# A third of the gated layer's seven products computed by halves, and the guard's maxima replaced by sums of squares on ScalarE

## The chip, the cores and the metric

The kernel runs on one core of a Trainium2 chip. A core has TensorE (PE in the profile; its weight loads are PEld), VectorE (DVE), ScalarE (ACT), GpSimd (POOL) and SyncE (SP), each with an instruction queue of its own, and 16 DMA engines that the queues of SP, ACT and POOL feed. The metric is the device time of one execution in microseconds (us), the median of the runs.

## The reference

Attention in which a query sees only the keys whose 6 hash bits equal its own, then a layer with a squared ReLU, in float32:

```
mask   = q_bucket[:, :, :, None] == k_bucket[:, :, None, :]     # 4 x 8 heads, 768 x 768
scores = where(mask, q @ k.T / 8, -1e9)
x      = softmax(scores) @ v        # as 3072 tokens x 512
h      = x @ w_in                   # 512 x 2048
g      = max(h, 0) ** 2
out    = g @ w_out                  # 2048 x 512
```

## The kernel before

All engines work in the order in which the program is written (a manual schedule); tile pools put in the waits. A tile name with `bufs=n` has n buffers, and a new tile of that name waits until an older one is done with.

**Attention** comes first (0 to 320.9 us). Its softmax leaves out the subtraction of the row's maximum. That is sound if scores stay small, so a guard looks at all of q and k: `load_peak` loads them in 32 pieces (through GpSimd's queue, two buffers `raw_qk`), `peak` takes the largest absolute value of each piece on VectorE, `tops` and `guard` reduce these, and a slow general path at the end is taken if the bound fails.

**The layer** runs over three chunks of 1024 tokens. Both of its products are matrix products by halves: each operand is cut in 2 x 2 blocks, and seven products of blocks, or of sums and differences of blocks, stand for the eight plain ones. The seven are numbered 0 to 6 in the code (`at(0)` to `at(6)`), and their results are added up in this way: "one" is product 0, "two" is 0 + 4, "five" is 3, "three" is "two" + 5; the four blocks of the result are 0 + 1, "two" + 3 + 6, "three" + "five", and "three" + product 2. TensorE adds in its accumulators (`acc0`, `acc1`, `acc2`, two buffers each), ScalarE copies what has to be kept on the way (`keep`: one, two, three, five), and VectorE adds (`gate_sum`) and makes the squared ReLU (`gated`).

*First layer, chunk 0* (`hidden`, 320.9 to 417.2 us): eight units r, each of seven products of two matmuls with 512 columns.

*First layer, chunks 1 and 2* (`hidden_pair`): the eight units are taken in four pairs; pair n holds units n (half 0) and n + 4 (half 1). Products 0, 3, 4, 5, 6 of each unit are "outer" matmuls with 512 columns, two for each product. Products 1 and 2 are computed for both units of a pair at once, by halves once more: seven "inner" matmuls with 256 columns take the place of eight such. `inner_steps` makes the steps 0 to 3 of an inner product and `put`, which adds it to a kept sum and gates it; `snaps` holds its kept copies. The inner weights are made once, in chunk 0's second layer, by `factor_units`, stored in `w_in_49`, and loaded by `load_inner`; `sums_inner` makes the differences of x. `load_unit` loads the outer weights. After each half, VectorE makes differences of the results (`minus` into `b_t` and `b12`), after each pair a slice of those for the second layer (`inner_sums(0, ...)`), and two `peak`s.

*Second layer* (`project`, k = 0 to 6): seven outer products, each of seven inner ones (`product`), each of these four matmuls with 256 columns on a quarter of `b11` ... `b_t`, with weight tiles `leaf` (seven buffers, loaded through ScalarE's queue). In `product` the groups go in the order 0, 1, 4, 3, 5, 6, 2. Group 4 needs `t2` of `inner_sums`, and the last one ("t4") needs `y21 - t2`, which VectorE makes in `hook`, called after the second group. The order around the change on VectorE in chunk 0 is: the sums of `factor_units(k - 1)` for k = 1 to 4, `hook`, the adds of the seven results (`first_`, `seventh`, ...), then differences for later k. `factor_units` loads its two sources and stores its results through GpSimd's queue, in tiles named `h` (five buffers), which the gating and `put_out` use too. `put_out` stores results mainly through SP's queue.

The functions in the code:

Of the kernel before, what the change touches and what calls it, by code (L numbers as in the profile page):

```python
# [34 lines left out]
def kernel(  # L35
# [49 lines left out]
    w_in_49 = p_d.tile([NQ, P, 2, 7, P], FP32, name="w_in_49")  # L85
# [572 lines left out]
    with tc.manual_schedule():  # L658
# [168 lines left out]

        def product(n, w, at, bt, c11, c12, c21, c22, hook=None):
# [47 lines left out]
        def peak(i):  # L876

            nc.vector.tensor_reduce(  # L878
                out=peaks[:, :, i], in_=raw_qk.pop(i), axis=AXL.X, op=ALU.max,
                apply_absolute_value=True,  # L880
            )
# [9 lines left out]
        def guard():  # L891
# [3 lines left out]
            for w in range(2):  # L895
# [8 lines left out]
                out=slow, in0=most[:, 0:1], scalar1=most[:, 1:2], scalar2=PLAIN / (scale * D),  # L904
# [52 lines left out]

        def factor_units(n):

            src = [new_h().rearrange("p (a f c) -> p a f c", a=2, c=P) for _ in range(2)]  # L960
            for j in range(2):
                nc.gpsimd.dma_start(out=src[j], in_=w_in_7[j * NQ + n, :, 5:7])
            sums = [new_h().rearrange("p (a f c) -> p a f c", a=2, c=P) for _ in range(2)]
            sums_a(
                src[0][:, :, 0], src[0][:, :, 1], src[1][:, :, 0], src[1][:, :, 1],
                *(sums[j // 2][:, :, j % 2] for j in range(4)),
            )
            for lo, hi, t in (
                (0, 2, src[0]), (2, 3, src[1][:, :, 1:2]), (3, 5, sums[0]), (5, 7, sums[1])
            ):  # L970
                nc.gpsimd.dma_start(out=w_in_49[n, :, :, lo:hi], in_=t)

        def load_inner(i, n):

            if n < NQ:
                w_inner[i, n] = []
                for j, name in enumerate((("sum0", "sum3"), ("sum2", "sum1"))[n % 2]):
                    t = p_y.tile([P, 4, QN], FP32, name=name).rearrange("p a (b c) -> p (a b) c", c=P)
                    nc.sync.dma_start(out=t[:, 0:7], in_=w_in_49[n, :, j])
                    w_inner[i, n].append(t)  # L980

        def quarters_x(i, j):

            b = xs[i][0][:, 2:4, 0:HN] if j == 0 else xs[i][0][:, 0:2, HN:NCH]
            return b[:, 0, 0:QN], b[:, 0, QN:HN], b[:, 1, 0:QN], b[:, 1, QN:HN]

        def sums_inner(i):

            t_inner[i] = [p_y.tile([P, NQ, QN], FP32, name=f"t{m}", bufs=2) for m in range(2)]
# [7 lines left out]
        def inner_steps(i, n, j):  # L997
# [5 lines left out]
            if i not in snaps:  # L1003
                o = [p_y.tile([P, HN], FP32, name="o", bufs=NOUT) for _ in range(2)]
                snaps[i] = [o[m // 2][:, m % 2 * QN:(m % 2 + 1) * QN] for m in range(4)]
            one, two, three, five = snaps[i]

            def mul(out, a, b, start, stop):
                nc.tensor.matmul(  # L1009
                    out=out, lhsT=w[:, a], rhs=b, start=start, stop=stop, skip_group_check=True  # L1010
                )
# [10 lines left out]
            def step_1():  # L1022
                hs["a2"] = spare("acc3")[:, 0, 0:QN]
# [24 lines left out]
        def hidden_pair(i, n, half):  # L1048

            r = half * NQ + n  # L1050
            w, bt = w_unit.pop(i * NR + 2 * n + half), factors_x(i)
            acc = {m: ps_m.tile([P, 512], FP32, name=f"acc{m}") for m in (0, 2)}

            def add(to, a, b, first, last):
                for f in range(NFT // 2):
                    nc.tensor.matmul(  # L1056
                        out=acc[to], lhsT=w[:, PLACE[a], f], rhs=bt[b](f),
# [4 lines left out]
            def keep(of, name):  # L1062
                t = p_r.tile([P, 512], FP32, name=name)
                nc.scalar.copy(out=t, in_=acc[of])
                return t

            if half == 0:
                load_inner(i, n + 1)
                now[0], now[1] = (inner_steps(i, n, j) for j in range(2))
            *steps, put = now[half]  # L1070
            add(0, 0, "11", True, False)
            one = keep(0, "one")
            if half:
                now[0][4](1, b11[:, r], one)
            else:
                steps[0]()
            add(2, 3, "t1", True, False)
            five = keep(2, "five")
            steps[1 - half]()
            add(0, 4, "t2", False, False)  # L1080
            two = keep(0, "two")
            steps[2 - half]()
            if half == 0:
                put(0, b11[:, r], one)
            add(2, 6, "22", False, True)
            gate_sum(b12[:, r], acc[2], two)
            steps[3 - half]()
            if half:
                put(0, b21[:, n], now["three"])
            add(0, 5, "t3", False, True)  # L1090
            three = keep(0, "three")
            gate_sum(b22[:, r], three, five)
            if half:
                steps[3]()
                put(1, b21[:, r], three)
            now["three"] = three
# [82 lines left out]
        def project(i):  # L1179
# [60 lines left out]
            for k in range(7):  # L1240
# [6 lines left out]
                if k == 6 and more:  # L1247
                    load_inner(i + 1, 0)
# [8 lines left out]
                def hook():  # L1257
# [4 lines left out]
                    if k == 6 and more:  # L1262
                        sums_inner(i + 1)
# [12 lines left out]
                )  # L1276
                if k in (3, 4) and i + 1 < NCHUNK:
# [59 lines left out]
        for i in range(NCHUNK):  # L1337
            for s in range(NR):
# [5 lines left out]
                minus(b_t[:, r], b12[:, r], b11[:, r])  # L1344
# [264 lines left out]
```

## Time and profile before

| what | us |
|---|---|
| median of 3 runs | 868.96 (868.72 to 869.63) |
| the profiled execution | 869.21 |
| its span, first to last instruction | 867.3 |
| attention, to the first unit | 320.9 |
| first layer, chunk 0 (320.9 to 417.2) | 96.3 |
| second layer, chunk 0 (417.2 to 502.6) | 85.4 |
| first layer, chunk 1 (502.6 to 596.0) | 93.4 |
| second layer, chunk 1 (596.0 to 680.2) | 84.2 |
| first layer, chunk 2 (680.2 to 773.0) | 92.8 |
| second layer, chunk 2 (773.0 to 859.6) | 86.6 |

The granted TensorE clock was 0.997 of full speed on average. A row of the timeline has the start, the length, the engine, the line, the operation, its tiles and shape and a count (neighbours of one kind are merged); in brackets stands how long the engine was idle before and what ended that. A float32 matmul is two records of PE. A record's length is longer than the distance from its start to the next, since matmuls overlap; the same holds for VectorE's.

### The profile page before, as it was taken

The page shows a single profiled execution, that of the slowest core. Times are in us where ns is not written, and L with a number is a line of the kernel's source. Part 1 is how long each engine was busy: PE and PEld are TensorE (multiplying, and loading weights), DVE is VectorE, ACT ScalarE, POOL GpSimd, SP SyncE. Part 2 cuts the span into 40 slices and gives each one's busy share as a digit, 9 for nine tenths or more (in the row PEclk, how much of TensorE's full clock was granted, in tenths as well). Part 3 has the DMA queues.
Part 4 walks back from the last instruction along what each step waited for, and adds up shares of the span by engine and source line. Part 5 has one row for each costly group of instructions (what it writes and reads, how often), then busy time and mean ns, then how long its engine had stood idle before and what let it go on. Part 6 is the DMA issues. An engine that isn't in the chain of part 4 may idle for free.

```text
span 867.3 us, 16734 instructions
## 1 busy us (share of the span) xinstructions
PE 854.5 (99%) x6548; PEld 520.4 (60%) x6548; DVE 749.5 (86%) x1005; ACT 361.9 (42%) x648; POOL 183.1 (21%) x346
## 2 busy tenths in 40 slices
PE   8999999999999999999999999999999999999996
PEld 3544444444444444444788865557888655568885
DVE  5799999999999988998779978888889688888875
ACT  5787777788877752222111123332111233321110
POOL 1332222223322201652132111112000111100002
PEclk9999999999999999999999999999999999999998
DMA  9677899879998527999788865537758645355565
GB/s 206 127 139 151 177 176 203 192 168 249 249 222 223 167 68 258 319 308 298 279 287 258 187 158 175 171 112 254 260 150 189 158 168 170 117 167 160 147 182 100
DMA packets 226629, 168.03 MB, mean 194 GB/s; under 512 B 167112, under 2 KB 184848, under 8 KB 226544
## 3 DMA queue, kind: packets, MB, share of 16 engines
q1 hardware_dynamic: 187744, 87.19, 40.9%
q0 software_dynamic: 16416, 41.95, 15.7%
q10 hardware_dynamic: 22384, 37.76, 14.6%
q8 instruction: 53, 0.87, 0.4%
q14 instruction: 32, 0.26, 0.1%
HBM read 124.52 MB, written 41.68 MB: 192 GB/s over the span
## 4 chain that ended last, share of the span: by engine, by line
PE 96%; DMA 2%; DVE 1%; issue 0%; ACT 0%; POOL 0%; POOLq 0%; DVEq 0%; ACTq 0%
PE acc L837 39%; PE st L430 18%; PE acc L1056 16%; PE xo L486 14%; PE acc L1009 6%; PE tot L535 2%; PE hash L360 1%; DMA leaf<-w_out 1%; DMA bits<-signed 1%; PE xo L337 0%; DVE total L473 0%; PE tp L320 0%; POOL bits L396 0%; DVE bits L410 0%; ACT feat L327 0%
## 5 line engine op out<-in xcount | busy, mean ns | idle before, releaser
L436 ACT ACTIVATE e<-st 128x768 f32<-128x768 f32 x192 | 155.4, 810 | 62.4 <-PE st L430 59.2
L430 PE MATMUL st<-feat 64*64 64x384 f32 x1536 | 158.1, 483 | 1.0 <-DVE feat L329 1.0
L486 PE MATMUL xo<-e,v_nat 64*64 64x385 f32 (+1 forms) x1520 | 158.7, 485 | 0.0
L837 PE MATMUL acc<-b,leaf 128*128 128x256 f32 x600 | 133.4, 379 | 0.3 <-DMA leaf<-w_out 0.3
L837 PEld LDWEIGHTS acc<-b,leaf 128*128 128x128 f32 x600 | 113.6, 190 | 17.2 <-issue 1.4
L473 DVE TENSOR_TENSOR total<-total,e 128x1536 f32<-128x1536 f32 x64 | 111.8, 1746 | 4.4 <-ACT e L436 2.8
L486 PEld LDWEIGHTS xo<-e,v_nat 64*64 64x64 f32 (+1 forms) x1520 | 56.4, 133 | 69.9 <-issue 52.8
L1056 PE MATMUL acc<-t_x,w_unit 128*128 128x512 f32 x192 | 90.2, 592 | 0.0
L430 PEld LDWEIGHTS st<-feat 64*64 64x64 f32 x1536 | 57.3, 133 | 38.1 <-issue 33.5
L837 PE MATMUL acc<-t,leaf 128*128 128x256 f32 x336 | 76.2, 380 | 0.0
L837 PEld LDWEIGHTS acc<-t,leaf 128*128 128x128 f32 x336 | 63.7, 190 | 9.1 <-DVE t L594 0.5
L921 DVE SCALAR_TENSOR_TENSOR b<-h 128x512 f32<-128x512 f32 x96 | 65.7, 691 | 3.0
L430 PE MATMUL st<-bits 64*64 64x384 bf16 x768 | 65.8, 325 | 1.1 <-DMA bits<-signed 1.0
L396 POOL DMA_DIRECT2D bits<-signed x120 | 61.5, 520 | 23.2 <-ACT signed L385 22.8
L1056 PE MATMUL acc<-x,w_unit 128*128 128x512 f32 x128 | 60.1, 592 | 0.0
L481 POOL MEMSET token<- 1x1 f32 x62 | 14.6, 236 | 206.0 <-PE xo L486 155.9
L837 PE MATMUL acc<-x,w_unit 128*128 128x512 f32 x128 | 56.5, 593 | 0.0
L1056 PEld LDWEIGHTS acc<-t_x,w_unit 128*128 128x128 f32 x192 | 36.5, 190 | 28.9 <-issue 26.8
L837 PE MATMUL acc<-b_t,leaf 128*128 128x256 f32 x240 | 53.8, 379 | 0.0
L1154 POOL DMA_DIRECT2D out_dram<-h x26 | 16.8, 654 | 174.1 <-DVE h L1147 167.1
L874 POOL DMA_DIRECT2D raw_qk<-in_q_dram x32 | 17.3, 541 | 162.4 <-DVE peaks L878 162.4
L837 PEld LDWEIGHTS acc<-b_t,leaf 128*128 128x128 f32 x240 | 45.5, 190 | 6.2
(156 smaller groups left out, 1206.6 us busy)
## 6 DMA issues: line engine op xcount, KB each, us to landing
leaf<-w_out ACTq DMA_DIRECT2D x142, 256.0 KB, 3.2
w_unit<-w_in SPq DMA_DIRECT2D x16, 640.0 KB, 4.0
raw<-in_moe_w_in_dram SPq DMA_DIRECT2D x8, 1024.0 KB, 6.8
raw<-in_moe_w_out_dram SPq DMA_DIRECT2D x8, 1024.0 KB, 7.4
w_unit<-w_in SPq DMA_DIRECT2D x8, 896.0 KB, 8.6
w_out<-sums POOLq DMA_DIRECT2D x16, 448.0 KB, 7.9
sum<-w_in SPq DMA_DIRECT2D x16, 448.0 KB, 5.0
v_nat<-in_v_dram SPq DMA_DIRECT2D x16, 384.0 KB, 5.3
```

The costliest lines, as they stand in the source:

```text
L396: nc.gpsimd.dma_start(out=t[h * D:h * D + NBITS + 1, w, c * HS:(c + 1) * HS], in_=signed[at:at + NBITS + 1, h],)
L430: nc.tensor.matmul(out=st[k * HK:(k + 1) * HK, h, 0:HS], lhsT=src[1][rows, key], rhs=src[0][rows, cut], start=first, stop=not first, skip_ ...
L436: nc.scalar.activation(out=key_of(pr, kt)[:, :, i, 0:HS], in_=st[:, :, 0:HS], func=ACTF.Exp, scale=scale)
L473: nc.vector.tensor_tensor(out=totals[pr], in0=totals[pr], in1=e, op=ALU.add)
L486: return nc.tensor.matmul(out=outs[pr][h * D:(h + 1) * D, c, 0:HS + 1], lhsT=nat[pr, "v_nat"][rows, h, kt * D:(kt + 1) * D], rhs=key_of(pr ...
L535: done = nc.tensor.matmul(out=spares[pr][g * 32:(g + 1) * 32, c2, 0:QS], lhsT=ones[rows], rhs=totals[pr][rows, h, c, c2 * QS:(c2 + 1) * QS ...
L837: nc.tensor.matmul(out=acc[to], lhsT=a(i), rhs=b(i), start=first and i == 0, stop=last and i == n - 1, skip_group_check=True,)
L874: nc.gpsimd.dma_start(out=raw_qk[i][:, w], in_=flat[:, i * n:(i + 1) * n])
L921: nc.vector.scalar_tensor_tensor(out=out, in0=h, scalar=0.0, in1=h, op0=ALU.max, op1=ALU.mult)
L1009: nc.tensor.matmul(out=out, lhsT=w[:, a], rhs=b, start=start, stop=stop, skip_group_check=True)
L1056: nc.tensor.matmul(out=acc[to], lhsT=w[:, PLACE[a], f], rhs=bt[b](f), start=first and f == 0, stop=last and f == NFT // 2 - 1, skip_group_ ...
L1154: queue.dma_start(out=out[at, m0 + a * 32:m0 + (a + 1) * 32].rearrange("(c i) j -> i c j", i=32), in_=ot[a * 32:(a + 1) * 32].rearrange("i ...
```

## The change

Product 6 of the paired units is now computed by halves too, as a third inner product. The steps of the three (A for product 1, B for product 6, C for product 2) are laid between the outer products over both halves of a pair, with two of them in flight at once. Their kept copies alternate between two sets, their accumulators come from `acc1` and `acc2` and from one tile `acc3` kept through the chunk. What product 6 adds to is now "two" + "five", an add on VectorE. The weights of B are made by `factor_third`, behind product k of chunk 0's second layer; the sources are loaded by `factor_units`. B's weights come in two tiles of the `leaf` pool. The differences of the results move to the places called `rest`. "two" and "five" have one buffer instead of two. The guard's `peak` becomes a square with a sum along each piece, on ScalarE, for q and k apart, at four places in each half; the guard's bound is changed to match. `load_inner` for the next chunk moves from ahead of product k = 6 into its `hook`.

```diff
-    w_in_49 = p_d.tile([NQ, P, 2, 7, P], FP32, name="w_in_49")
+    w_in_49 = p_d.tile([NQ, P, 3, 7, P], FP32, name="w_in_49")
@@ load_unit
-            m = 7 if n < NR else 5
+            m = 7 if n < NR else 4
@@ product, keep
+        KEPT = dict(one=2, two=1, three=2, five=1)
-                t = p_r.tile([P, 512], FP32, name=name)[:, 0:w]
+                t = p_r.tile([P, 512], FP32, name=name, bufs=KEPT[name])[:, 0:w]
@@ peak
-            nc.vector.tensor_reduce(
-                out=peaks[:, :, i], in_=raw_qk.pop(i), axis=AXL.X, op=ALU.max,
-                apply_absolute_value=True,
+            t = raw_qk[i][:, w]
+            nc.scalar.activation(
+                out=t, in_=t, func=ACTF.Square, accum_out=peaks[:, w, i:i + 1]
             )
@@ factor_units
+            thirds[n] = new_h().rearrange("p (j f c) -> p j f c", j=2, c=P)
+            for j in range(2):
+                nc.gpsimd.dma_start(out=thirds[n][:, j], in_=w_in_7[j * NQ + n, :, PLACE[6]])
...
+        def factor_third(n):
+
+            src = thirds.pop(n)
+            sums = new_h().rearrange("p (m c) -> p m c", c=P)
+            sums_a(
+                src[:, 0, 0], src[:, 0, 1], src[:, 1, 0], src[:, 1, 1],
+                *(sums[:, m] for m in range(4)),
+            )
+            for lo, hi, t in (0, 2, src[:, 0]), (2, 3, src[:, 1, 1:2]), (3, 7, sums):
+                nc.gpsimd.dma_start(out=w_in_49[n, :, 2, lo:hi], in_=t)
@@ load_inner
+                ts = [p_y.tile([P, NQ, P], FP32, name="leaf", bufs=NLEAF) for _ in range(2)]
+                for m, t in enumerate(ts):
+                    hi = min(4 * m + 4, 7)
+                    nc.sync.dma_start(out=t[:, 0:hi - 4 * m], in_=w_in_49[n, :, 2, 4 * m:hi])
@@ sums_inner: three sets of differences, not two
+                p_y.tile([P, NQ, QN], FP32, name=f"t{m}", bufs=2 - m // 2) for m in range(3)
@@ inner_steps
+                snaps[i] = o, [t_inner[i][m][:, 3] for m in range(3)], spare("acc3")
+            side = (3 * n + (0, 2, 1)[j]) % 2
+            one, two, five = snaps[i][side]
+            three = one
+            last = snaps[i][2][:, side, 0:QN]
-                a0, a1 = (ps_m.tile([P, 512], FP32, name="acc1")[:, 0:QN] for _ in range(2))
+                a0, a1 = (ps_m.tile([P, 512], FP32, name=f"acc{m}")[:, 0:QN] for m in (1, 2))
@@ hidden_pair, the order of steps (A, B, C: the inner products; [4]: put)
+            def rest(r):
+                minus(b_t[:, r], b12[:, r], b11[:, r])
+                minus(b12[:, r], b22[:, r], b12[:, r])
+            add(acc, 0, "11", True, False)
+            one = keep(acc, "one")
+            if half == 0:
+                A[0]()
+            else:
+                B[2]()
+                C[0]()
+                A[4](1, b11[:, r], one)
+                B[4](0, b12[:, r0], now["two"])
+            mark()
+            other = ps_m.tile([P, 512], FP32, name="acc2")
+            add(other, 3, "t1", True, True)
+            five = keep(other, "five")
+            if half == 0:
+                A[1]()
+            else:
+                B[3]()
+                C[1]()
+                rest(r0)
+            mark()
+            add(acc, 4, "t2", False, False)
+            two = keep(acc, "two")
+            if half == 0:
+                A[2]()
+                B[0]()
+                A[4](0, b11[:, r], one)
+                nc.vector.tensor_tensor(out=two, in0=two, in1=five, op=ALU.add)
+            else:
+                C[2]()
+                nc.vector.tensor_tensor(out=two, in0=two, in1=five, op=ALU.add)
+                B[4](1, b12[:, r], two)
+                C[4](0, b21[:, r0], now["three"])
+            mark()
+            add(acc, 5, "t3", False, True)
+            three = keep(acc, "three")
+            if half == 0:
+                A[3]()
+                B[1]()
+                gate_sum(b22[:, r], three, five)
+            else:
+                C[3]()
+                gate_sum(b22[:, r], three, five)
+                C[4](1, b21[:, r], three)
+                rest(r)
+            mark()
@@ project
-                if k == 6 and more:
-                    load_inner(i + 1, 0)
...
                     if k == 6 and more:
+                        load_inner(i + 1, 0)
                         sums_inner(i + 1)
...
+                if i == 0 and 0 < k <= NQ:
+                    factor_third(k - 1)
@@ the loop over chunks and units: the two differences and peak only where rest and mark don't make them
-                minus(b_t[:, r], b12[:, r], b11[:, r])
+                if i == 0:
+                    minus(b_t[:, r], b12[:, r], b11[:, r])
...
-                minus(b12[:, r], b22[:, r], b12[:, r])
+                if i == 0:
+                    minus(b12[:, r], b22[:, r], b12[:, r])
                 for n in range(2):
                     m = 2 * ((i - 1) * NR + s) + n
-                    if m >= 0:
-                        peak(m)
```

More of the change, by code (lines that the diff above doesn't have):

```diff
@@ L1048, in hidden_pair @@
         def hidden_pair(i, n, half):
[L1050 removed]
+            r0, r = n, half * NQ + n
             w, bt = w_unit.pop(i * NR + 2 * n + half), factors_x(i)
[L1052 removed]
+            acc = ps_m.tile([P, 512], FP32, name="acc0")
             def add(to, a, b, first, last):
@@ L1062, in keep, with mark @@
             def keep(of, name):
-                t = p_r.tile([P, 512], FP32, name=name)
-                nc.scalar.copy(out=t, in_=acc[of])
-                return t
+                t = p_r.tile([P, 512], FP32, name=name, bufs=KEPT[name])
+                nc.scalar.copy(out=t, in_=of)
+                return t
+            marks = iter([(2 * ((i - 1) * NR + 2 * n + half) + m, c) for m in range(2) for c in range(2)])
+            def mark():
+                peak(*next(marks))
+            def rest(r):
+                minus(b_t[:, r], b12[:, r], b11[:, r])
+                minus(b12[:, r], b22[:, r], b12[:, r])
@@ L1081, in hidden_pair @@
-            two = keep(0, "two")
-            steps[2 - half]()
-            if half == 0:
[L1084 to L1095, printed above, removed]
@@ L1099 @@
+            mark()
[11 more added lines that the diff above has]
+            mark()
+            now["two"], now["three"] = two, three
         OUTER = (0, b11), (5, b12), (3, b_t), (6, b22), (1, b21), (4, b11), (2, b_t)
```

39 lines of the change are left out of this document (16 added, 23 removed).

## The prediction

> **What bounds the kernel now.** I read the page first, then the busy times by stage, then the timeline of PE alone through one pair, then of VectorE, GpSimd and PE around the places that the change touches.
>
> ```profile
> PE 854.5 (99%) x6548; PEld 520.4 (60%) x6548; DVE 749.5 (86%) x1005; ACT 361.9 (42%) x648; POOL 183.1 (21%) x346
> ...
> PE 96%; DMA 2%; DVE 1%; issue 0%; ACT 0%; POOL 0%; POOLq 0%; DVEq 0%; ACTq 0%
> ```
>
> TensorE sets the time, so a matmul less is worth its length, but only where nothing else becomes late. By stage (columns: stretch, length, then busy time and instructions of PE, PEld, DVE, ACT, POOL; clock; DMA share, GB/s), first chunk 0's second layer, then chunk 1's pairs:
>
> ```profile
> 417.20:502.60 85.40, 85.06 (x393) 74.16 (x392) 77.77 (x120) 11.75 (x31) 21.52 (x33) 1.00 0.86 260
> 502.60:596.00 93.40, 93.40 (x276) 52.17 (x275) 75.11 (x128) 31.14 (x72) 14.92 (x28) 1.00 0.51 162
> ```
>
> In the pairs PE has no gap, VectorE 18 us of slack and ScalarE 62. In chunk 0's second layer VectorE is busy 91% and DMA 86%: the place to distrust. PE within a pair (start, length, the group's form):
>
> ```profile
> 680.20 1.88 PE L1056 MATMUL acc<-x,w_unit 128*128 128x512 f32 x4
> 681.91 1.03 PE L1009 MATMUL acc<-x,sum 128*128 128x256 f32 x4
> 682.78 1.88 PE L1056 MATMUL acc<-t_x,w_unit 128*128 128x512 f32 x4
> ```
>
> Starts give the price: four records of 512 columns take 1.72 us (0.43 each), four of 256 take 0.86 (0.215). A matmul is two records.
>
> **Step 1, PE's gain.** A pair loses product 6 in both halves, 8 records x 0.43 = 3.44 us, and gets 7 matmuls = 14 records x 0.215 = 3.01. That is 0.43 us a pair, x 8 pairs = **-3.4 us**, the whole that can be gained.
>
> **Step 2, work moved between engines.** VectorE loses the 32 maxima:
>
> ```profile
> L878 DVE TENSOR_REDUCE peaks<-raw_qk 128x2 f32<-128x768 f32 x32 | 28.9, 947 | 0.0
> ...
> L1064 ACT COPY two<-acc 128x512 f32<-128x512 f32 x16 | 9.4, 585 | 24.4 <-PE acc L1056 24.4
> ```
>
> and gets, a pair, three adds of 256 and two of 512 columns (0.34 and 0.60 from start to start), 2.2 us x 8 = 18. As PE waited for none of this, the lighter VectorE is worth 0 here. ScalarE gets 64 squares of 128x384: between its copies of 256 (0.37) and its ACTIVATE of 512 with a bias tile (0.72); I take 0.55. Four a half (2.2 us of 11.4) fit its idle time; behind each in its queue stand copies that PE needs 1 us later or more, so a square late by 1 us would start to cost. Its data lands in 3.3 us (at most 6.9) and is asked for about 11 us ahead. The weights of the new inner product are loaded on SP's queue, behind a leaf that is just done; 5.0 us to land, due 7.8 us into the pairs: 0. Unit loads shrink by 128 KB: 0. Single buffers for "two" and "five": the closest case in chunk 0 is a "two" last read at 348.77 and written again at 350.49, 1.7 us to spare: 0.
>
> **Step 3, a short distance.** In the second half of a pair only two matmuls of 256 (0.86 us) stand between the fourth outer product and the one that goes on in the same bank, which must wait for the copy "two". ScalarE starts such a copy 0.2 us after (756.71 to 756.90), takes 0.585; then 0.06 to a waiting weight load (as 777.76 to 777.82 below) and 0.2 for that load: 1.05. So 0.19 us a pair, **+1.5 us**; from 0 to 0.4 a pair.
>
> **Step 4, the tail of each chunk's pairs.** The second layer's third group needs the inner differences of the last pair, the last thing VectorE does there:
>
> ```profile
> 776.89 0.42 DVE L594 TENSOR_TENSOR t<-b 128x256 f32<-128x256 f32 x1
> 777.34 0.42 DVE L594 TENSOR_TENSOR t<-b,t 128x256 f32<-128x256 f32 x1
> 777.68 0.42 DVE L594 TENSOR_TENSOR b<-b 128x256 f32<-128x256 f32 x1
> 777.82 2.02 PEld L837 LDWEIGHTS acc<-t,leaf 128*128 128x128 f32 x10 [0.27 <-DVE t L594]
> ```
>
> Pairs end at T = 773.04; the last slice is due at T+4.5 and was ready at T+4.8. Afterwards VectorE can begin its tail only at T-1.95, when product C's sixth matmul is read: two adds 0.68, the new add of "five" 0.60, four add-and-gate steps at 1.33, both differences of b_t and b12 1.2 (one used to come later), two inner ones 0.87. That is 8.67, so ready at T+6.7: a wait of 2.0 us where 0.13 stood, twice: **+3.7 us** (1.2 to 2.5 each). The maxima that go used to come after this point.
>
> **Step 5, chunk 0's second layer.** Each product's last group (t4) needs a difference that VectorE makes behind the sums of factor_units; their sources are loaded through GpSimd's in-order queue:
>
> ```profile
> 438.16 1.41 POOL L971 DMA_DIRECT2D w_in<-h x2 [4.32 <-DVE h L590]
> 439.29 1.39 POOL L962 DMA_DIRECT2D h<-w_in x2
> ```
>
> ```profile
> 446.67 0.43 DVE L588 TENSOR_TENSOR h<-h 128x256 f32<-128x256 f32 x1 [3.87 <-DMA h<-w_in]
> ...
> 463.21 1.22 DVE L594 TENSOR_TENSOR b<-b,t 128x1024 f32<-128x1024 f32 x1
> ```
>
> ```profile
> 461.18 8.80 PE L837 MATMUL acc<-b,leaf 128*128 128x256 f32 x40
> ```
>
> VectorE already stood 3.87 us for that load in product 2; and in product 3 its difference ends at 464.43, when t4's weight load is due (461.18 + 16 records x 0.215 - 0.2 = 464.42): no slack at all. Now factor_third puts its sums behind product k on VectorE and its store on GpSimd, ahead of the next loads. Its four ops of 128 columns: 0.21, or 0.32 after a dependence, continued from the 512 and 256 rows, 1.0 us. In times of this trace:
>
> Product 2: product 1's last add ends at 442.8, third sums 443.8, store 0.7, two loads 1.4: issued by 445.9 instead of 440.7. Earlier loads landed 4.8 to 6.0 us after their issue ended; with 5.4, VectorE goes on at 451.3. Sums 1.47 and difference 1.2: 454.0, due 452.3. PE late by 1.7.
> Product 3: VectorE needs the same 17.8 us as from 446.67 to 464.43, plus 1.0: 470.1, due 464.4. Late by 5.7 in all.
> Product 4: adds 4.55 and third sums 1.0: 475.7; store and loads 2.1, landing 5.4: 483.2 (VectorE had nothing else from 478.1); sums and difference 2.7: 485.9, due 476.5. Late by 9.4.
> Product 6: its difference ended at 498.62, 24.6 after product 4's; with 1.0 more, 511.6, due 500.7. Late by 10.9. **+10.9 us**; 9.7 to 12.1 by the landing.
>
> [...] The row of this case is 6.2 (issue to landing), at a DMA share of 0.86:
>
> ```profile
> h<-w_in POOLq DMA_DIRECT2D x8, 256.0 KB, 6.2
> ```
>
> **Step 6, chunk 1's start.** PE begins at 502.6 + 10.9 = 513.5. VectorE now makes 12 inner differences where 8 took 3.2: 511.6 + 4.75 + two adds 0.8 + 0.42 = 517.6, when bank acc2 of the last product is read. Inner step 0 now takes an acc2 buffer, so the outer product behind it needs this one, at 515.9: **+1.7 us** (0 to 2.7). Into chunk 2 VectorE read that bank at 679.37, before PE's start at 680.20; 1.6 later still does: 0.
>
> Sum: the profiled execution's 869.2 - 3.4 + 1.5 + 3.7 + 10.9 + 1.7 = 883.6; the median lies 0.25 lower, so **883.3 us**, slower by 1.7%.
>
> **Rivals.** (a) Faster: PE's 3.4 us are kept. It decides if third sums and loads are done before the differences are due (loads landing within about 1 us, or not queued behind the store) and if the tail ends by T+4.8. For: PE-bound everywhere, lighter VectorE in the pairs. Against: steps 4 and 5's rows. 865.5; with step 3, 867.0.
> [...]
> (c) Loads not delayed at all, VectorE's extra work alone, with product 2's wait swallowing the first third: 1.1 in place of 10.9: 873.5. Against: the two GpSimd lines above, loads right behind a store that waited.
> (d) The two PE gaps of step 5 (4.0 and 3.7 us; the longest here is 0.8) drop the granted clock, 1.00 in every stage so far. [...]
> (e) Only the tail and the short distance count, and cancel the gain: about 870.5, no change that can be told.
> That inner matmuls cost more than half of outer ones, so that nothing is saved, the 0.215 and 0.43 exclude.
>
> **Chances.** Forecast 0.56, (a) 0.12, (b) 0.12, (c) 0.08, (d) 0.07, (e) 0.05. What a measurement of this kernel can tell is about 0.2%: faster 0.12, same 0.05, slower 0.83. Forecast with its bounds (9.7 to 12.1, 0 to 2.7, 0 to 3, 2.4 to 5): 878 to 889. Range 871 to 889, which takes in (b), (c), (d) and leaves out (a), most of (e).
>
> **What would show it.** In the profile after: VectorE's wait on h<-w_in in product 2 longer than 5 us and a second one in product 4; PEld at L837 waiting for b and b_t of L594, some 10 us in all; loads at GpSimd directly behind the store of third sums; about 2 us of PEld waiting for t at the head of chunks 1 and 2's second layer; pairs of 23.0 us instead of 23.3. Wrong would be step 5 if chunk 0's second layer stays at 85.4 us, and the whole if PE's busy gaps sum to under 3 us.

## The result, and the profile after

The changed kernel takes 884.34 us (median of 4 runs, 882.73 to 887.1), the kernel before 869.3 (868.72 to 869.74) beside it: a ratio of 1.0176 (95% interval 1.0157 to 1.0195), slower by 1.8%. The profiled execution took 884.65 us, its span 882.9.

The lengths of the stages below run from PE's first record of a stage to that of the next, for both kernels. The table of the kernel before has 93.4 and 84.2 us for chunk 1, as it puts the border at 596.0; PE's first record of that second layer is at 595.46, which gives the 92.84 and 84.74 used here.

| stage | before | after | difference |
|---|---|---|---|
| attention, to the first unit | 320.94 | 319.89 | -1.05 |
| first layer, chunk 0 | 96.24 | 96.24 | 0 |
| second layer, chunk 0 | 85.43 | 94.58 | +9.15 |
| pairs of chunk 1 | 92.84 | 95.93 | +3.09 |
| second layer, chunk 1 | 84.74 | 88.60 | +3.86 |
| pairs of chunk 2 | 92.84 | 91.51 | -1.33 |
| second layer, chunk 2 | 85.99 | 88.13 | +2.14 |
| end of the span | 8.31 | 8.01 | -0.30 |

The differences add up to the spans' 15.55. Attention and the end are the same code in both; their 1.35 is variation from run to run. First the page's busy time and the shares of the chain that ended last, the lines that answer to the first ones of before:

```profile
PE 859.8 (97%) x6596; PEld 532.5 (60%) x6596; DVE 749.9 (85%) x1037; ACT 409.2 (46%) x816; POOL 194.4 (22%) x366
...
PE 89%; DVE 5%; DMA 3%; issue 1%; POOL 0%; ACT 0%; DVEq 0%; SPq 0%; POOLq 0%
```

PE's share of the chain fell from 96% to 89%; VectorE has 5% of it and DMA 3%. PE is busy 5.3 us *longer* than before, although it has fewer columns to compute: that is the first sign of a lower clock (0.989 on average, where the kernel before has 0.997). The busy times by stage (columns as before: length, PE, PEld, DVE, ACT, POOL, clock, DMA share, GB/s) say where:

```profile
416.12:510.71 94.59, 88.88 (x394) 76.20 (x393) 79.60 (x130) 11.78 (x31) 32.15 (x53) 0.96 0.83 257
510.71:606.64 95.93, 93.47 (x297) 56.41 (x296) 75.17 (x141) 53.60 (x153) 16.74 (x31) 0.98 0.56 178
606.64:695.24 88.60, 86.56 (x393) 75.57 (x392) 76.36 (x111) 12.36 (x34) 7.00 (x11) 0.98 0.66 194
695.24:786.75 91.51, 91.51 (x297) 55.91 (x296) 72.18 (x132) 53.48 (x153) 15.03 (x28) 1.00 0.51 165
```

Only the pairs of chunk 2 (the last line) are without a gap, at a granted clock of 1.00 and shorter than before. In chunk 0's second layer GpSimd is busy 32 us where it was 21.5, and VectorE 1.8 us more. GpSimd's rows around the first third (start, length, operation, count, idle time before and what ended it):

```profile
442.88 0.54 POOL L989 DMA_DIRECT2D w_in<-h  x1 [3.56 <-DVE h L591]
443.41 1.08 POOL L966 DMA_DIRECT2D h<-w_in  x2
```

The store of the third's sums (L989) keeps the queue standing for VectorE, and the loads of the next units (L966) leave directly behind it, at 443.41; before, they left at 439.29, and the changed kernel runs some 1.1 us ahead here. VectorE then waits, once in product 2 and once in product 4:

```profile
450.09 0.42 DVE L588 TENSOR_TENSOR h<-h 128x256 f32<-128x256 f32 x1 [7.51 <-DMA h<-w_in]
...
480.54 0.42 DVE L588 TENSOR_TENSOR h<-h 128x256 f32<-128x256 f32 x1 [3.66 <-DMA h<-w_in]
```

PE stands for the differences that follow, and after the longer gap, of 3.67 us, it runs at half speed, at a granted clock of 0.50. First PE's rows, then VectorE's around the two differences, then the busy times of the stretches from 466 us on (the column behind POOL is the granted clock):

```profile
452.88 1.97 PE L839 MATMUL acc<-b_t,leaf 128*128 128x256 f32 x8 [1.33 <-issue]
...
468.88 8.46 PE L839 MATMUL acc<-b,leaf 128*128 128x256 f32 x24 [3.67 <-issue]
```

```profile
451.56 1.22 DVE L594 TENSOR_TENSOR b_t<-b_t,t 128x1024 f32<-128x1024 f32 x1
452.70 1.22 DVE L594 TENSOR_TENSOR t<-b 128x1024 f32<-128x1024 f32 x1
...
467.56 1.22 DVE L594 TENSOR_TENSOR b<-b,t 128x1024 f32<-128x1024 f32 x1
468.70 0.42 DVE L1192 TENSOR_TENSOR tmp<-acc,one 128x256 f32<-128x256 f32 x1
```

```profile
466.00:468.90 2.90, 0.02 (x1) 0.05 (x1) 2.87 (x7) 0.00 (x0) 1.41 (x2) 0.88 0.80 288
468.90:472.00 3.10, 3.10 (x8) 2.47 (x8) 2.93 (x8) 0.00 (x0) 1.15 (x3) 0.50 0.65 215
472.00:475.00 3.00, 3.00 (x9) 2.37 (x8) 2.77 (x9) 0.00 (x0) 0.22 (x1) 0.50 0.02 5
475.00:477.20 2.20, 2.20 (x12) 1.94 (x11) 1.84 (x2) 0.37 (x1) 2.20 (x5) 0.99 0.59 150
```

The profile puts both of PE's gaps down to "issue". What ended them is read from the times: each time PE goes on 0.18 us after VectorE passes from the difference to its next operation (452.70 to 452.88, 468.70 to 468.88).

In the two middle stretches 8 and 9 records fit where full clock fits 14 (0.215 us each), at a granted clock of 0.50. The 24 records took 8.46 us; 24 records took 5.42 at full clock with the store on SP's queue. No later gap stands in product 4: PE used up there, at half speed, time in which it would have waited for VectorE's second late load. A third gap, of 0.48 us, stands ahead of the last group of product 6.

The heads of the second layers of chunks 1 and 2:

```profile
613.59 3.29 PE L839 MATMUL acc<-t,leaf 128*128 128x256 f32 x10 [2.04 <-DVE t L594]
616.68 9.66 PE L839 MATMUL acc<-b,leaf 128*128 128x256 f32 x40
...
793.70 2.42 PE L839 MATMUL acc<-t,leaf 128*128 128x256 f32 x10 [2.04 <-DVE t L594]
795.96 8.80 PE L839 MATMUL acc<-b,leaf 128*128 128x256 f32 x40
```

Both have the same wait of 2.04 us for the last slice of the inner differences. But in chunk 1 the 50 records behind it take 1.73 us more (0.87 and 0.86) than in chunk 2. The granted clock of the stretches behind the two waits:

```profile
613.60:616.90 3.30, 3.30 (x11) 2.79 (x12) 3.27 (x4) 0.37 (x1) 0.00 (x0) 0.71 1.02 412
616.90:618.50 1.60, 1.60 (x5) 1.24 (x5) 1.60 (x3) 0.37 (x1) 0.00 (x0) 0.53 1.01 383
...
793.70:796.00 2.30, 2.30 (x11) 2.04 (x12) 2.30 (x5) 0.37 (x1) 0.00 (x0) 1.00 0.21 38
```

Then the start of chunk 1's pairs:

```profile
510.71 1.88 PE L1086 MATMUL acc<-x,w_unit 128*128 128x512 f32 x4
515.04 1.17 PE L1039 MATMUL acc<-x,sum 128*128 128x256 f32 x4 [2.46 <-DMA sum<-w_in]
516.01 3.58 PE L1086 MATMUL acc<-t_x,w_unit 128*128 128x512 f32 x4
```

PE waits 2.46 us for inner weights, and four records of 512 columns then take 3.58 us where 1.88 is usual: half clock again (granted 0.50 from 516.00 to 519.40 us), 1.70 lost. At last a second half of a pair, where the distance between the fourth outer product (759.07) and the one that goes on in its bank (761.64) is short:

```profile
759.07 1.88 PE L1086 MATMUL acc<-t_x,w_unit 128*128 128x512 f32 x4
760.78 1.03 PE L1039 MATMUL acc<-x,sum 128*128 128x256 f32 x4
761.64 1.96 PE L1086 MATMUL acc<-t_x,w_unit 128*128 128x512 f32 x4
763.44 0.59 PE L1039 MATMUL acc<-t,sum 128*128 128x256 f32 x2
```

From start to start the group at 761.64 takes 1.80, not 1.71: the short distance costs 0.09 us a pair.

### The profile page after: what moved, and what is told of

Same layout as the page of the kernel before. It is cut to its first block, busy times and chain, and to the rows that moved or that the text cites. A ratio compares the mean times of both kernels' runs of the same rounds, so it can differ in the third digit from the quotient of the medians.

```text
span 882.9 us, 17000 instructions
## 1 busy us (share of the span) xinstructions
PE 859.8 (97%) x6596; PEld 532.5 (60%) x6596; DVE 749.9 (85%) x1037; ACT 409.2 (46%) x816; POOL 194.4 (22%) x366
## 4 chain that ended last, share of the span: by engine, by line
PE 89%; DVE 5%; DMA 3%; issue 1%; POOL 0%; ACT 0%; DVEq 0%; SPq 0%; POOLq 0%
PE acc L839 34%; PE st L430 18%; PE xo L486 14%; PE acc L1086 12%; PE acc L1039 8%; PE tot L535 1%; PE hash L360 1%; DMA leaf<-w_out 1%; DVE t L594 1%; DMA sum<-w_in 1%; DVE b L923 1%; DVE b L594 1%; DMA h<-w_in 1%; PE xo L337 1%; DVE h L1073 0%
## 5 line engine op out<-in xcount | busy, mean ns | idle before, releaser
L839 PE MATMUL acc<-b,leaf 128*128 128x256 f32 x600 | 137.3, 387 | 3.8 <-issue 3.7
L839 PEld LDWEIGHTS acc<-b,leaf 128*128 128x128 f32 x600 | 116.7, 195 | 21.6 <-issue 4.5
L1086 PE MATMUL acc<-t_x,w_unit 128*128 128x512 f32 x192 | 92.6, 605 | 0.0
L839 PE MATMUL acc<-x,w_unit 128*128 128x512 f32 x128 | 56.5, 593 | 0.0
L846 ACT COPY two<-acc 128x256 f32<-128x256 f32 (+1 forms) x29 | 12.5, 432 | 92.8 <-PE acc L839 73.6
L846 ACT COPY one<-acc 128x256 f32<-128x256 f32 (+1 forms) x29 | 12.5, 432 | 84.1 <-PE acc L839 59.9
```

Of the source, the lines that this page charges most:

```text
L839: nc.tensor.matmul(out=acc[to], lhsT=a(i), rhs=b(i), start=first and i == 0, stop=last and i == n - 1, skip_group_check=True,)
L1086: nc.tensor.matmul(out=to, lhsT=w[:, PLACE[a], f], rhs=bt[b](f), start=first and f == 0, stop=last and f == NFT // 2 - 1, skip_group_check ...
```

## Experiments

All ratios are to the kernel before on the same chip: 869.82 us for the first four runs, 869.87 for the others. The theory throughout: the lost time is made of separate costs, each a wait of PE for VectorE that the new work has made late.

### The third's store on SP's queue

```diff
@@ factor_third
-                nc.gpsimd.dma_start(out=w_in_49[n, :, 2, lo:hi], in_=t)
+                nc.sync.dma_start(out=w_in_49[n, :, 2, lo:hi], in_=t)
```

> The three stores of the third factors go through SP's queue instead of GpSimd's; all else is the changed kernel. Theory (the next loads of factor_units stand behind a store that waits for VectorE): loads are issued right behind the stores of factor_units, about 4 us earlier, VectorE's 7.5 us wait in product 2 falls to about 4, the second one (3.7 us) goes; chunk 0's second layer falls from 94.6 to about 88 us, the kernel from 884.3 to about 877. Rival one (the four VectorE operations of each third, 1 us, are what costs, or the added DMA traffic): the layer stays within 1 us of 94.6 and the kernel of 884.

Measured: 877.63 us (4 runs), ratio 1.0102 (1.0072 to 1.0131), so 0.0074 or 6.4 us less than the changed kernel. The profiled execution (876.19) is one of the two shorter of the four (875.6 to 881.19), so its stages give more, 8.6. Chunk 0's second layer takes 88.84 us (94.58 in the changed kernel), chunk 1's pairs 93.08 (95.93). The same places, GpSimd's queue and VectorE:

```profile
438.28 0.57 POOL L966 DMA_DIRECT2D h<-w_in  x1
440.38 0.55 POOL L966 DMA_DIRECT2D h<-w_in  x1 [1.52 <-DMA w_in<-h]
```

```profile
445.48 0.43 DVE L588 TENSOR_TENSOR h<-h 128x256 f32<-128x256 f32 x1 [3.11 <-DMA h<-w_in]
```

The first load leaves 5.1 us earlier and VectorE's wait falls from 7.51 to 3.11; the one for the loads of product 4 is gone (it waits 2.34 us there, for a buffer that is being stored). So some two thirds of this stage's loss is the place of the third's stores in GpSimd's queue, ahead of the next loads; of the three for each product it is the last, that of the sums, that waits. What is left is 3.4 us: PE's gaps are now 1.34, 0.60 and 1.11 us, in products 3, 4 and 6. No run splits them up. In the rows, each third's sums still take 0.93 us of VectorE's time, four times, and both GpSimd's second load (the 1.52 above) and VectorE (the 2.34) wait for a buffer that an earlier store is still reading.

### The third's sums on GpSimd

```diff
@@ sums_a, with an engine as argument
-        nc.vector.tensor_tensor(out=s1, in0=a21, in1=a22, op=ALU.add)
+        by.tensor_tensor(out=s1, in0=a21, in1=a22, op=ALU.add)
...
@@ factor_third
-                *(sums[:, m] for m in range(4)),
+                *(sums[:, m] for m in range(4)), by=nc.gpsimd,
```

> The four sums of each third factor run on GpSimd instead of VectorE; all else is the changed kernel. Theory: GpSimd needs no word from VectorE at the product's end, so the next loads are issued about 2 us behind the stores of factor_units, and VectorE is 4 us lighter: chunk 0's second layer about 87 us, the kernel about 876. Rival one of the operations themselves: the same direction, by 4 us at most (880). Rival two (DMA traffic): 884.

Measured: 880.05 us (4 runs), ratio 1.0122 (1.0105 to 1.0139); chunk 0's second layer 91.56. It is a gain, but smaller than I expected, and the time is the 880 of rival one, by which only the operations themselves cost. The rows speak against that rival: the third's store no longer waits for VectorE, yet GpSimd's own work stands ahead of the loads:

```profile
437.67 0.47 POOL L589 TENSOR_TENSOR h<-h 128x128 f32<-128x128 f32 x1
...
439.71 1.64 POOL L990 DMA_DIRECT2D w_in<-h  x3
441.34 1.08 POOL L967 DMA_DIRECT2D h<-w_in  x2
```

Behind product 2 its four sums even take 0.89, 1.44, 1.44 and 0.45 us. VectorE still waits for the loads, twice (5.87 and 3.79 us), and PE's longest gaps, 2.26 and 1.84, come behind these waits. Both runs agree in this: it matters when the next loads leave, and what is ahead of them. What the lighter VectorE is worth beside that isn't told apart.

### The inner differences earlier

The slice of the inner differences is made behind the first unit's differences of the last half, no longer behind the whole pair.

```diff
@@ hidden_pair, second half
                 rest(r0)
+                inner_sums(0, slice(n, n + 1))
@@ the loop over units
-                if i > 0 and s % 2:
-                    inner_sums(0, slice(s // 2, s // 2 + 1))
```

> inner_sums of the last layer's first product is called right behind rest(r0) in a pair's second half instead of at the end of the pair; all else is the changed kernel. Theory (VectorE's tail holds up the second layer's third group): the 2.0 us waits of PE at the head of the second layer of chunks 1 and 2 go, and any loss of clock behind them: 884.3 to about 880 (4 us from the waits, up to 2 more from the clock). Rival (VectorE is late as a whole there and the wait turns up in the next group or product): 884 within 1 us, with waits of PE on VectorE of the same sum elsewhere in that layer.

Measured: 877.0 us (4 runs), ratio 1.0075 (1.0058 to 1.0092), so 8.8 us less than the changed kernel, more than I expected. The second layers of chunks 1 and 2 take 84.61 and 85.83 us, a little less than before the change, with no gap:

```profile
605.47 3.62 PE L839 MATMUL acc<-b,leaf 128*128 128x256 f32 x16
608.92 3.62 PE L839 MATMUL acc<-t,leaf 128*128 128x256 f32 x16
612.38 8.80 PE L839 MATMUL acc<-b,leaf 128*128 128x256 f32 x40
```

That is 6.3 us, most of it the two waits of 2.04 and the clock that had fallen behind one of them. In the profile a further 2.4 lie at chunk 1's start, where the wait for the inner weights was 1.76 us this time and the four records of 512 columns behind it took the usual 1.88. The edit doesn't touch that start, so I take this part for variation between runs, which isn't shown. The rows fit it: PE had the inner weights 3.64 us into the pairs (511.93 to 515.57), against 4.33 in the changed kernel (510.71 to 515.04).

### The short distance lengthened

```diff
@@ hidden_pair, second half
-                B[3]()
                 C[1]()
                 rest(r0)
             mark()
             add(acc, 4, "t2", False, False)
...
+                B[3]()
                 C[2]()
```

> Step 3 of product B moves from ahead of the fourth outer product to behind it in a pair's second half; all else is the changed kernel. Theory (outer product 5 waits for the copy two because only 0.86 us lie between): the 8 waits of 0.2 us at a weight load on ACT two go, pairs shorten by 0.09 us each, 0.7 us in all. Rival (ScalarE is late by its squares, not by the distance): the waits stay.

Measured: 882.86 us in one run. Weight loads no longer wait for "two", and the pairs of chunk 2 take 91.19 us, not 91.51: 0.08 a pair, 0.64 for eight. From the whole time of one run no more can be read.

### The third's work moved to the first layer

`factor_third`'s loads go through SP's queue in units 4 and 6 of chunk 0's first layer, into the guard's two idle buffers; the sums are made in units 5 and 7, where VectorE has idle time, and stored through SP's queue. Nothing else is changed.

```diff
@@ hidden (chunk 0's first layer)
+            def hook():
+                for n in ((0, 1) if r == 5 else (2, 3) if r == 7 else ()):
+                    factor_third(n)
+            for n in ((0, 1) if r == 4 else (2, 3) if r == 6 else ()):
+                load_third(n)
@@ project
-                if i == 0 and 0 < k <= NQ:
-                    factor_third(k - 1)
```

> The changed kernel with the third's loads, sums and stores alone moved into chunk 0's first layer, as in the run with all three costs taken out; the tail and the short distance stay as changed. My theory: second layer of chunk 0 back from 94.6 to 85.4 (-9.2), chunk 1's start loses its wait of 2.5 us for the inner weights or most of it, and the clock no longer falls there (-1.7); the heads of the later second layers still cost 2.0 us each and up to 0.5 to 1.5 of clock. Whole: 884.3 less 9.2 less 2.5 to 4.2: 871 to 872.6. Rival A (GpSimd's queue was only part of it: VectorE is behind by itself in that layer, by the lack of the two inner differences' slack or the store traffic): second layer 87 to 89, whole 874 or more. Rival B (the wait for the inner weights at chunk 1's start is of its own, SP's queue behind the output stores): second layer 85.4, but the wait of 2.5 us stays, and whole 875.

Measured: 873.22 us (7 runs), ratio 1.0040 (1.0029 to 1.0052), 11.8 us less than the changed kernel. The difference is within what my theory gave (11.7 to 13.4); the time itself is 0.6 over its 871 to 872.6. The second layer of chunk 0 takes 86.44 us, not 85.4, with a gap of 1.59 us in product 3; the pairs of chunk 1 take 91.84. The wait for the inner weights is gone, though these still come through SP's queue behind the output stores:

```profile
502.90 1.88 PE L1096 MATMUL acc<-x,w_unit 128*128 128x512 f32 x4
504.84 1.13 PE L1049 MATMUL acc<-x,sum 128*128 128x256 f32 x4
```

So rival B falls: that wait isn't a cost of its own. SP's rows show the link. Issues of `sum<-w_in`, ahead of the pairs' first record, came 4.3 us early before the change (498.36), 1.9 in the changed kernel and 3.2 in this run, since the 16 stores ahead of them in SP's queue wait for VectorE's results of chunk 0. The later VectorE is against PE, the later these weights are asked for. The landing counts as well: it took 7.0 us in the changed kernel, 5.3 before the change, and with the store on SP's queue, where the weights came 2.2 us early but landed in 5.2, PE waited only 0.25. Why it took 7.0 isn't shown. The changed kernel:

```profile
489.12 19.42 SPq L1213 DMA_DIRECT2D out_dram<-h  x16
508.78 0.88 SPq L997 DMA_DIRECT2D sum<-w_in  x2
```

### All three costs taken out

The last edit, together with the earlier inner differences and the lengthened distance (point (iii) of the expectation: as in the run that did this alone, the step comes one place later).

> The changed kernel with all three costs taken out at once. (i) The third's sources are loaded through SP's queue in units 4 and 6 of chunk 0's first layer, into the two buffers of the guard's pieces, which are free by then; they are summed on VectorE in units 5 and 7, in its idle time, and stored through SP's queue, so that nothing of factor_third is left in the second layer or in GpSimd's queue. (ii) The tail of a chunk's pairs makes the inner differences slice by slice behind each pair, and (iii) step 3 of inner product B goes one place earlier, as in the runs that did one of these alone. My theory (three separate costs: chunk 0's second layer, the heads of the second layers, the short distance, and a start of chunk 1 that follows from the first): chunk 0's first layer 96.2, its second layer 85.4 (94.6 in the changed kernel, 85.4 before), chunk 1's pairs 91.2 to 92.5 (up to 1.3 us for a bank or the inner weights at the start), chunk 2's pairs 91.2, second layers 84.6 and 85.9 for chunks 1 and 2. Whole: 869.3 before less 3.1 for the fewer matmuls, plus up to 1.3: 866 to 867.5, ratio 0.997. Rival A (VectorE and the DMA queues have no room anywhere for the third's work, so the cost only moves): units 4 to 7 of chunk 0 lengthen by 3 us or more, or the second layer stays over 88; whole at or above 869. Rival B (the costs aren't separate; something else in the pairs eats the matmuls' gain): pairs of chunk 2 at 92.5 or more, whole 868.5 to 870.

Measured: 866.22 us (5 runs), ratio 0.9959 (0.9946 to 0.9973): faster than both kernels, and 0.4% below the one before, with an interval that lies below 1. By stage, as above:

```profile
417.06:503.34 86.28, 84.84 (x393) 74.40 (x392) 77.75 (x119) 11.76 (x31) 23.98 (x37) 1.00 0.87 266
503.34:594.54 91.20, 91.20 (x298) 56.24 (x297) 73.55 (x138) 53.33 (x153) 16.06 (x30) 1.00 0.56 180
594.54:679.14 84.60, 84.60 (x393) 74.48 (x392) 75.50 (x109) 12.31 (x34) 7.00 (x11) 1.00 0.69 202
```

Both stages of pairs take 91.19 us from start to start, where they took 92.84: 0.41 us for each of eight pairs, the matmuls' gain and nothing less. Both rivals fall: the third's work fits elsewhere, with 0.5 us lost in chunk 0's first layer (96.74 us, a wait of 0.24 for weights among it), and nothing else eats the gain. Chunk 0's second layer is still 0.85 over before, by one gap of 1.44 us in product 3: VectorE waited 5.58 us for h<-w_in in product 2, against 3.87 before. The prediction found no slack in that product; here a transfer that landed later than before showed it. Why it landed later isn't shown.

The savings of the separate runs, 11.8, 8.8 and 0.64, add up to 21.2 us; together they are 18.9. The 2.4 us at chunk 1's start are in both the 11.8 and the 8.8, which accounts for the rest.

### The squares alone

The kernel before, with its maxima replaced by squares on ScalarE, at the old place.

```diff
@@ peak, in the kernel before
-            nc.vector.tensor_reduce(
-                out=peaks[:, :, i], in_=raw_qk.pop(i), axis=AXL.X, op=ALU.max, ...)
+            for w in range(2):
+                t = raw_qk[i][:, w]
+                nc.scalar.activation(
+                    out=t, in_=t, func=ACTF.Square, accum_out=peaks[:, w, i:i + 1]
+                )
```

> The kernel before, with one part of the change alone: the guard's maxima on VectorE become squares with sums on ScalarE (two of 128x384 for each piece... the same 64 activations as in the changed kernel), at the place where the maxima stood, behind each pair. My theory (step 2 of the prediction: work off VectorE is worth nothing, since PE waits for none of it, and ScalarE has room): ratio 1.000, within 0.002; pairs 92.84 as before. Rival A (ScalarE's longer queue delays a copy that frees a bank: four squares in a row take 4 x 0.72 = 2.9 us, and a copy that PE needs stands behind them): each pair lengthens by up to 1.5 us, so up to +12 us, visible as waits of PE for ACT. Rival B (a lighter VectorE does shorten something, the heads of the second layers): 0.13 us each, -0.3 us, not to be told from none.

Measured: 871.24 us (11 runs), ratio 1.0016 (1.0007 to 1.0025). That is 1.4 us more than before: the ratio is inside the 0.002 that I allowed, but the pairs don't stay at 92.84, and rival A is right in kind: the pairs of chunk 1 take 94.15 us and those of chunk 2 93.87 (92.84 before), with one wait in the last pair of each. The timeline there:

```profile
583.72 0.58 ACT L1065 COPY three<-acc 128x512 f32<-128x512 f32 x1 [1.34 <-PE acc L1057]
583.73 2.54 ACTq L1124 DMA_DIRECT2D leaf<-w_out  x5
...
586.37 0.52 ACT L880 ACTIVATE raw_qk<-raw_qk 128x384 f32<-128x384 f32 x1 [2.06 <-issue]
...
588.41 0.56 ACT L1065 COPY one<-acc 128x512 f32<-128x512 f32 x1
...
589.02 1.99 PE L1057 MATMUL acc<-t_x,w_unit 128*128 128x512 f32 x4 [1.04 <-ACT one L1065]
```

ScalarE issues five leaf loads (2.54 us) in the last pair, then four squares in a row, each with a read of its sum (2.04 us in all), and only then the copy that PE waits for. In the earlier pairs, without the leaf loads, the four squares cost PE nothing. In the changed kernel the squares stand one by one at four places of a half, and the pairs of the run with all costs taken out have no such wait. No run has the leaf loads and four squares in a row apart from each other in that pair, so it is the two together that are shown to cost.

### The maxima back on VectorE

The run with all three costs taken out, but with the guard as before the change: two maxima on VectorE behind each half of a pair.

```diff
@@ peak
-        def peak(i, w):
+        def peak(i):
-            nc.scalar.activation(out=t, in_=t, func=ACTF.Square, ...)
+            nc.vector.tensor_reduce(..., op=ALU.max, apply_absolute_value=True)
```

> The run with all three costs taken out, but the guard's maxima back on VectorE (the other part of the change undone), two behind each half of a pair. This asks whether the move of the guard to ScalarE was needed for the seven matmuls in place of eight. My theory (VectorE has 18 us of slack in a stage of pairs; the adds of the third inner product take 9 of it and the maxima 15 more, 24 against 18): this is tight; VectorE falls behind in the pairs by 6 us a chunk at the most, and I expect 2 to 6 us over the run with the squares, as PE waits for VectorE's adds to release banks or at the head of the second layers. Rival (the maxima fit, as VectorE's busy share counts overlapped records and its real slack is larger): within 0.5 us of the run with the squares, so the move bought nothing.

Measured: 867.52 us (6 runs), ratio 0.9972 (0.9960 to 0.9984). The pairs take 91.19 us in both chunks, exactly as with the squares: VectorE's extra work costs nothing there, and my 6 us a chunk are refuted. The second layers of chunks 1 and 2 are 0.77 and 0.74 us longer in the profile. In chunk 1 there is a wait of 0.25 for a leaf. In chunk 2 PE stands 0.49 us, until 793.73, for a difference that VectorE ends at 793.55; the last pair's two maxima, 1.80 us, now come ahead of it. So VectorE's lateness does reach PE at that place, with half a microsecond. Chunk 0's second layer is 0.73 shorter. The medians lie 1.3 us apart, less than my 2 to 6, but the intervals overlap, so whether the move of the guard is worth 1.3 us or nothing stays open. The pairs' gain doesn't need it.

## Why the prediction was right, and where not

Forecast were 883.3 us, measured 884.34. The step that carries it (step 5) and its mechanism are shown. In the steps' own terms, for the profiled executions:

| step | predicted | measured | from |
|---|---|---|---|
| 1, matmuls | -3.4 | -3.3 | 8 x 0.41, all costs taken out |
| 2, moved work | 0 | 0 | pairs of that run without a gap |
| 3, short distance | +1.5 | +0.65 | 8 x 0.08, distance lengthened |
| 4, tail | +3.7 | +4.3 | 2.14 in chunk 2, and 3.86 less 1.73 of clock in chunk 1 |
| 5, chunk 0's second layer | +10.9 | +9.15 | stages, the clock behind the long gap within it |
| 6, chunk 1's start | +1.7 | +2.7 | 95.93 less 91.51, less 1.70 of clock |
| clock (rival d) | not in the sum | +3.4 | 1.73 and 1.70 |
| attention, end | 0 | -1.35 | same code in both |

That the two sums agree to about 1 us is in part luck: steps 3 and 5 were put 2.6 us too high, steps 4 and 6 1.6 too low, the clock's 3.4 weren't in the sum, and attention and the end happened to take 1.35 less.

Rivals (a), (c) and (e) fall with chunk 0's second layer: they leave it at the 85.4 of before or, in (c), 1.1 above, and it took 94.58.

**Step 3** was mis-sized: PE loses 0.08 a pair, not 0.19. The trace shows the weight loads waiting 0.2 us each, eight times, for "two"; less than half of that reaches PE. I put in 0.2 us for the load itself; by the rows the matmul starts at 761.64, 0.02 after the load that waited (761.62).

**Step 4** is right by place, size and cause: 2.04 us against the 2.0 worked out, twice, and gone where the differences are made earlier.

**Step 5** is right in its mechanism: a late load, behind a store that waits, makes VectorE late, and VectorE makes PE late. Of its lateness figures, product 2's 1.7 was 1.33 by the gap, and product 3's 5.7 in all was 5.0 (1.33 + 3.67). The term that was too large is the landing in product 4. From the end of the loads' issue to VectorE's going on I put 5.4 us in; it was 5.6 in product 2 (444.49 to 450.09), but 4.15 in product 4 (476.39 to 480.54), so that product 4 added less. The sign that I named was some 10 us of PE waiting: it waits 5.5 us (1.33, 3.67 and 0.48), and 3.04 of the rest is the half speed behind the second gap.

Rival (b), that these loads land much faster than step 5 has it, is not what the runs show: their median from issue to landing is 5.0 us in the changed kernel (4.2 between 440 and 482 us), 6.2 before the change, and 5.1 to 6.0 in the six other runs whose rows list them.

**Step 6** has about the right size by the wrong mechanism. I put the wait on the bank acc2 and set the inner weights at 0; it was the inner weights, late behind output stores in SP's queue (16 of them stood ahead before the change too, so the later place of `load_inner` in the program moved it past none). The step that failed is the sentence in step 2 that counts their 5 us against the 7.8 into the pairs: that holds for the third's own weights, while the ones that were late are needed first, 1.7 us into the pairs. These were asked for 1.9 us ahead of the pairs and took 7.0 us to land, not 5.0. The bank's wait shows only where those weights come sooner: 0.78 us with the store on SP's queue, 0.25 with the distance lengthened.

**Rival (d)** had a chance of 0.07 and came true beside the forecast, with more to it than I gave: the clock fell behind gaps of 2.04 and 2.46 us too. Where it followed the long gap, of 3.67, it was nearly free, since PE would have waited for VectorE anyway: VectorE ends product 4's difference at 483.14, and PE comes to the group that needs it at about 484.1, so under 1 us of the 3.04 lost can have mattered, and PE waits for VectorE again in product 6. Where it followed the gaps of 2.04 and 2.46 us, nothing hid it, and it cost 1.7 each.

**Step 2** holds for the change as written but not as a rule: work off VectorE was worth nothing that could be told, but ScalarE's 62 us of idle time did not make four squares in a row free wherever they stand. In three pairs of four they were; in the last, behind the leaf loads, they cost PE 0.76 and 1.04 us. Spaced out, as in the change, they cost nothing that the pairs show.

## What to carry to other kernels

Before saving matmuls on a PE-bound kernel, follow the preparation of the new operands through every queue: here 3.3 us were won in the matmuls and some 20 lost, most of it because a store that waits for its data stood ahead of the next loads, and because one slice was made at the end of a stage though its inputs were there long before. The same work, put where its engines are idle, kept the whole gain of the pairs and cost 1.35 us in chunk 0. A PE gap of 2.0 to 2.1 us was followed by another 1.73 us lost to the clock in four cases of ten, so here small gaps of a busy PE were worth removing too.

## What the runs showed of the hardware

**The clock fell behind some short gaps and not behind others.** In this change's runs the wait of 2.0 to 2.1 us at the head of a second layer occurs ten times (five profiles, two each). Four times the 50 records behind the wait took 1.73 us more, each time the same; six times they did not. In the changed kernel the two cases stand side by side: granted clock 0.71 and 0.53 in the stretches from 613.60 and 616.90 us, 1.00 from 793.70. The lost 1.73 agrees with these two clocks: 3.30 us at 0.71 and 1.60 us at 0.53 leave out 1.71 us, by estimate. The other gaps of PE in the layer, as far as the rows show what came behind them: none of 1.84 us or less was followed by a drop, nor the one of 2.26; the one of 2.46 was, with 0.50 over the 3.40 us from 516.00, and so was the one of 3.67 in the changed kernel, with 0.50 from 468.90 to 475.00 us. Why the clock fell behind some of these gaps of 2.0 to 2.1 us and not behind others isn't shown. Whether it is behind the spread of the changed kernel's times (0.5%, where before has 0.1% beside it) is open; it can't be the whole of it, as executions of 887.1 and 884.03 us have the same mean granted clock, 0.991.

**A square with a sum is two instructions on ScalarE**: 532 ns for 128x384 and 197 ns for reading the sum, 64 of each in the changed kernel. They overlap: in the run of the squares alone four in a row take 2.04 us from start to start, 0.51 each. The prediction took 0.55 us for the whole, which is right by that measure.
